# Second feed-forward stage: coefficients in fewer passes, slopes for eight chunks at once, late range marks, idle products, new order

## The chip, the cores and the metric

The kernel runs on one core of a Trainium2 chip. The metric is device time in microseconds (us) of one execution; the kernel before was timed in three runs. TensorE (PE) multiplies; VectorE (DVE), ScalarE (ACT) and GpSimd (POOL) work element by element; SyncE (SP) issues the transfers.

## The reference

Attention over 4 batches of 8 heads (576 tokens, masks of two kinds), then a soft mixture of 8 experts, then a feed-forward layer. The change is in the last of them, on 2304 tokens of width 512:

```
h = x @ w_in                      # x 2304 x 512, w_in 512 x 2048 (float64)
g = h - np.tanh(h)
return (g @ w_out).astype(np.float32)   # w_out 2048 x 512 (float64)
```

Here x is c @ slot_out, with 32 slots, so that h is c times (slot_out @ w_in), and only 32 rows of that product are needed.

## The kernel before

The program has four parts, one after the other: attention (to about 145 us), the dispatch and the experts of the mixture (to about 199 us), and `second`, the feed-forward layer, which is what changes.

`second` reads w_in and w_out as 64-bit words, in 16 pieces i0..i15 (128 columns of w_in) and 16 pieces o0..o15 (128 rows of w_out), 512 KB each, in the order of the list `loads`. Eleven raw buffers take them; a later load waits until a buffer is free again. Each piece is turned into float32 by `low` (ACT or POOL, L774 and L776), `top` (POOL, L779) and `merge` (DVE, L783); `check` (DVE, L787) makes a range mark from it. A raw buffer is free when its merge and its check are done.

The 16 chunks of 128 hidden columns go in nine batches: [0], [1], then pairs. For each batch PE makes a tile p (one buffer): the product of w_in with the slots (L878), to which the marks of the i pieces and of the o pieces loaded so far are added (L883). ACT copies it to g (L887), PE makes the deviations and the means (L891 with `dev`, L893 with `devT`) back into p, ACT takes Gs from it (L898), DVE corrects Gs (L901) and copies GT (L904). Then p is free for the next batch. From GT, POOL makes the coefficients of the batch (`coeffs`, nine operations, L909 and L910) and one slope for each chunk (PT, L935).

The tokens are 18 tiles of 128, in phases: A (tiles 0 to 3), BG (4 to 7), EG (16, 17), C (8 to 11), DG (12 to 15). For each phase and chunk f: PE makes h (L996, 3 buffers), ACT squares it to u with coefficient SC (L1000), DVE makes r from h, u and coefficient BB (L1007, 4 buffers; now and then ACT and POOL, L1011 and L1015), and PE adds r times w_out to the tiles' accumulators acc (L976, 4 buffers), from the rounded copy whi (POOL L856 or ACT L857). Phase A is made while the pieces still arrive. `msum` (L943) sums the slopes times w_out over all chunks; after two more steps it is Ms, and every tile gets one more product with Ms ("affine"). The partial sums of phase A wait in `store` (L1041); their affine products come last of all, and L1059 adds and writes them.

A verdict on the range is worked out on DVE (`judge_b`, L1076 on, and `judge_c`) with one small product between (L1101); it sets a flag that is read at the end, for a slow path that doesn't run here.

The order of all this on each engine is set ahead of time by `Plan`: tasks with durations, dependencies and buffers, placed one by one; on the chip each engine runs its list strictly in order. The attention and the experts keep their own order.

Of the kernel before, what the change touches and what calls it, by code (L numbers as in the profile page):

```python
# [78 lines left out]
class Plan:  # L79

    def __init__(self, bufs):
        self.tasks, self.bufs = [], bufs

    def add(self, *alts, deps=(), take=(), free=(), ready=0.0):
        t = dict(alts=alts, deps=[d for d in deps if d is not None], take=take, free=free, ready=ready, id=len(self.tasks))
        self.tasks.append(t)
        return t

    def run(self, free_at):
        tasks, free_at = self.tasks, dict(free_at)  # L90
# [18 lines left out]

        def earliest(t):  # L110
            s = t["ready"]
            for d in t["deps"]:
                s = max(s, d["end"] + (0.05 if d["eng"] == t["alts"][0][0][0] else 0.2))
            for tag, key in t["take"]:
                k = order.get(tag, [])
                s = max(s, taken.get(tag, -99.0))
                if len(k) >= self.bufs[tag]:
# [3 lines left out]
                    s = max(s, released[old] + 0.1)  # L121
            return s

        while open_:
# [51 lines left out]
def attention_moe_moe(ctx: ExitStack, tc: tile.TileContext, q, k, v, phi, w1, w2, w_in, w_out, cst, out, dbg=None):  # L176
# [20 lines left out]
    big = const.tile([128, NS], F16, name="big")  # L197
    nc.gpsimd.memset(big, 2.0 ** 13)
# [538 lines left out]

    NCK = 8

    def second(raw, chk, cT, store, more):  # L740
# [3 lines left out]
        loads = pieces("i0 o0 i1 o1 i2 i3 o2 o3 i4 i5 o4 o5 i6 i7 o6 o7 i8 i9 o8 o9 i10 i11 o10 o11 i12 i13 o12 o13 i14 i15 o14 o15")  # L744
# [552 lines left out]
```

## Time and profile before

| | |
|---|---|
| three runs | 363.84, 365.88, 366.21 us; median 365.88 |
| the profiled execution | 367.04 us, of which 365.3 us is its span |
| PE, DVE, ACT, POOL busy | 310.7, 244.8, 182.6, 140.2 us |
| granted TensorE clock over the span | 0.919 of full speed |

Times in the trace count from the start of the span. A busy PE is not a PE at its peak, since the matmuls are pipelined and their ends are modelled; a row's idle time is that of its engine just before the instruction, and behind the arrow stands what ended it.

### The profile page before, as it was taken

What the parts mean: (1) busy time and instruction counts of PE and PEld (TensorE: products, weight loads), DVE (VectorE), ACT (ScalarE), POOL (GpSimd) and SP (SyncE); (2) the same over time, 40 slices, a digit from 0 to 9 for tenths busy, and PEclk for the clock granted to TensorE, in tenths of its full rate; (3) what the DMA queues carried; (4) which work ended last, traced back from release to release, by engine and by line L of the source; (5) the groups of instructions that cost most, each with busy time, mean ns of one, the idle gap of its engine ahead of it and who ended that gap; (6) DMA issues with size and microseconds to landing.
All of it is one profiled execution on the core that took longest, in us unless ns stands there. A gap on an engine that the chain in (4) does not pass through costs nothing.

```text
span 365.3 us, 7576 instructions
## 1 busy us (share of the span) xinstructions
PE 310.7 (85%) x2635; PEld 224.2 (61%) x2635; DVE 244.8 (67%) x786; ACT 182.6 (50%) x371; POOL 140.2 (38%) x263
## 2 busy tenths in 40 slices
PE   7996998799999998999997466474889999899990
PEld 4885887588788785643443344352664677676670
DVE  5696697478788875447227765966875568985552
ACT  3364565456586754322214466467265546666520
POOL 0555452636355420015006899989770000110000
PEclk9998899699999999999999655599699999999997
DMA  4677799697889999969999998532000003101106
GB/s 130 159 192 230 203 251 252 160 235 205 223 220 247 241 294 361 358 240 396 410 400 375 374 316 276 174 135 97 2 0 0 2 0 116 60 0 50 65 17 222
DMA packets 52988, 70.20 MB, mean 192 GB/s; under 512 B 22608, under 2 KB 40400, under 8 KB 52944
## 3 DMA queue, kind: packets, MB, share of 16 engines
q1 hardware_dynamic: 52944, 69.65, 60.2%
q8 instruction: 23, 0.38, 0.4%
q14 instruction: 21, 0.17, 0.1%
HBM read 64.91 MB, written 4.72 MB: 191 GB/s over the span
## 4 chain that ended last, share of the span: by engine, by line
PE 34%; POOL 13%; DVE 6%; issue 4%; ACT 1%; DVEq 0%; POOLq 0%; ACTq 0%
PE acc L976 15%; PE h L996 5%; PE hp L689 3%; PE sop L704 3%; POOL co L910 3%; POOL co L909 2%; POOL PT L935 2%; POOL X L779 2%; PE ht L696 2%; PE sp L611 1%; DVE r L1007 1%; PE msum L943 1%; POOL whi L856 1%; PE dt L584 1%; DVE chk_i L787 1%
## 5 line engine op out<-in xcount | busy, mean ns | idle before, releaser
L976 PE MATMUL acc<-whi,r 128*128 128x512 f32 x288 | 83.9, 412 | 4.9 <-DVE r L1007 3.0
L1000 ACT ACTIVATE u<-h,co 128x512 f32<-128x512 f32 (+1 forms) x80 | 51.0, 646 | 34.2 <-PE h L996 31.6
L1007 DVE SCALAR_TENSOR_TENSOR r<-h,co,u 128x512 fp32r<-128x512 f32 (+1 forms) x77 | 52.6, 694 | 19.4 <-PE acc L976 16.1
L976 PEld LDWEIGHTS acc<-whi,r 128*128 128x128 f32 x288 | 54.6, 196 | 17.5 <-DVE r L1007 3.3
L380 PE MATMUL sc<-kT,qbd 128*128 128x96 f32 x272 | 40.0, 288 | 0.5 <-DVE kT L311 0.2
L403 ACT COPY pT<-pp 96x512 f32<-96x512 f32 x38 | 22.2, 584 | 35.5 <-PE pp L402 35.1
L384 DVE CUSTOM_DVE_ANT_0 sm<-sc,m_sb 128x96 f32<-128x96 f32 x144 | 29.4, 260 | 14.8 <-PE sc L380 10.9
L380 PEld LDWEIGHTS sc<-kT,qbd 128*128 128x128 f32 x272 | 35.3, 200 | 3.1 <-issue 2.0
L996 PE MATMUL h<-cT,Gs 128*128 128x512 f32 (+1 forms) x80 | 33.8, 440 | 1.0 <-DVE r L1007 0.9
L255 POOL TENSOR_SCALAR qm<-q 72x512 f32<-72x512 f32 x30 | 20.0, 684 | 29.6 <-PE tr_k L295 11.5
L255 POOL TENSOR_SCALAR km<-k 72x512 f32<-72x512 f32 x30 | 19.6, 669 | 28.7 <-DMA k<-in_k 14.0
L413 PE MATMUL pv<-vw,pT 96*64 96x65 f32 x608 | 27.6, 232 | 3.1 <-POOL vw L278 2.8
L413 PEld LDWEIGHTS pv<-vw,pT 96*64 96x64 f32 x608 | 21.8, 140 | 9.7 <-issue 4.5
L402 PE MATMUL pp<-c_sb,sm 128*96 128x128 f32 x152 | 23.9, 281 | 0.7 <-ACT sm L395 0.7
L388 DVE TENSOR_TENSOR sm<-sm,mx 128x384 f32<-128x384 f32 (+1 forms) x38 | 23.6, 622 | 1.2
L996 PEld LDWEIGHTS h<-cT,Gs 128*128 128x128 f32 x80 | 15.3, 199 | 14.3 <-DVE r L1007 11.0
L1015 POOL TENSOR_TENSOR r<-d,u 128x512 fp32r<-128x512 f32 x3 | 4.3, 1436 | 50.7 <-ACT d L1011 50.7
L878 PE MATMUL p<-X,soT 128*32 128x256 f32 (+1 forms) x72 | 7.3, 488 | 18.3 <-DVE Gs L901 16.2
L395 ACT ACTIVATE sm<-sm 128x384 f32<-128x384 f32 x38 | 19.9, 523 | 3.7 <-DVE sm L388 3.0
L311 DVE COPY kT<-tr_k 128x288 f32<-128x288 f32 x32 | 17.8, 562 | 4.9 <-PE tr_k L295 4.8
L295 PE MATMUL tr_k<-c_sb,km 72*128 72x72 f32 x128 | 16.2, 251 | 5.3 <-POOL km L255 3.1
L302 ACT COPY qbd<-tr_q 64x288 f32<-64x288 f32 x32 | 13.3, 414 | 12.9 <-PE tr_q L295 12.7
(196 smaller groups left out, 583.1 us busy)
## 6 DMA issues: line engine op xcount, KB each, us to landing
w<-in_moe_w SPq DMA_DIRECT2D x60, 512.0 KB
raw_o<-in_moe_w_out SPq DMA_DIRECT2D x16, 512.0 KB
raw_i<-in_moe_w_in SPq DMA_DIRECT2D x15, 512.0 KB
q<-in_q SPq DMA_DIRECT2D x32, 144.0 KB
k<-in_k SPq DMA_DIRECT2D x32, 144.0 KB
out<-X SPq DMA_DIRECT2D x14, 256.0 KB
vw<-in_v SPq DMA_DIRECT2D x16, 144.0 KB
vw<-in_v SPq DMA_DIRECT2D x32, 64.0 KB
```

Of the source, the lines that this page charges most:

```text
L255: nc.gpsimd.tensor_scalar(out=dst, in0=src, scalar1=1.0, scalar2=0.0, op0=ALU.mult, op1=ALU.add)
L380: nc.tensor.matmul(sc[:, o:o + n, :].rearrange("p g k -> p (g k)"), lhsT=qbd[u % NQ][:, j].rearrange("p a n -> p (a n)"), rhs=keys, start= ...
L384: nc.vector.tensor_tensor_reduce(out=sm[:, o:o + n, :].rearrange("p g k -> p (g k)"), in0=sc[:, o:o + n, :].rearrange("p g k -> p (g k)"), ...
L388: nc.vector.tensor_tensor(out=sm[:, o:o + n], in0=sm[:, o:o + n], in1=mx[:, o:o + n].unsqueeze(2).to_broadcast([128, n, KB]), op=ALU.subtract)
L395: nc.scalar.activation(out=st[b], in_=st[b], func=AF.Exp, scale=0.125)
L402: nc.tensor.transpose(pp[:, i, :], sm[:, i, :], ident)
L403: nc.scalar.copy(pT, pp)
L413: nc.tensor.matmul(pv[64 * ab:64 * ab + 64, i, :], lhsT=pT[:, o + x, 64 * ab:64 * ab + 64], rhs=w[:, ab, u % 2, j + x, :], start=x == 0, s ...
L976: nc.tensor.matmul(live[key], lhsT=lhsT(), rhs=rhs(), start=new, stop=stop)
L996: nc.tensor.matmul(live["h", key], lhsT=Gs[:, 128 * f:128 * (f + 1)], rhs=cT[:, c0:c0 + w], start=True, stop=True)
L1000: nc.scalar.activation(out=live["u", key], in_=live["h", key], func=AF.Square, scale=co[:, SC, f:f + 1])
L1007: nc.vector.scalar_tensor_tensor(out=live["r", key], in0=live["h", key], scalar=co[:, BB, f:f + 1], in1=live["u", key], op0=ALU.add, op1=A ...
```

## The change

- **Coefficients.** `coeffs` has five POOL operations for a batch where there were nine. GT is copied by ACT, unclamped, where DVE copied and clamped it. Factors of 8, 5 and 1/8 go into `dev`, `devT`, SC, whi and the copies that are made anyway.
- **Slopes.** The 16 operations of L935 are replaced by two calls of `slope`, for eight chunks each: five small operations and two of 128x256.
- **Late marks.** The check of o8 to o15 moves behind Ms, with a product of its own for each piece (`marks`, eight of 128x512) and one reduction, ahead of `judge_b`.
- **Idle products.** In phase A four products of 128x512 that nobody reads go ahead of each h, into the same buffer.
- **Constants.** `dev`, `devT` and `big` are made when the loads start, in the tile `more`.
- **Order.** i8 to i15 are loaded ahead of o8 to o15; the planner has other durations and hand-over times, takes buffers in the order in which tasks were added, and has boosts; r has 5 buffers; the alternative of ACT and POOL for r is never taken (`POOLR`). The affine products of phase A go in between instead of last, and the last phase ends tile by tile.

```diff
-        loads = pieces("i0 o0 i1 o1 i2 i3 o2 o3 i4 i5 o4 o5 i6 i7 o6 o7 i8 i9 o8 o9 i10 i11 o10 o11 i12 i13 o12 o13 i14 i15 o14 o15")
+        loads = pieces("i0 o0 i1 o1 i2 i3 o2 o3 i4 i5 o4 o5 i6 i7 o6 o7 i8 i9 i10 i11 i12 i13 i14 i15 o8 o9 o10 o11 o12 o13 o14 o15")
...
+        dev, devT, big = more[:, 3 * DM:3 * DM + 128], more[:, 3 * DM + 128:3 * DM + 161], more[:, 3 * DM + 161:].bitcast(F16)
...
-        plan = Plan(dict(raw=RAW, chk=NCK, h=3, p=1, acc=4, u=3, r=4, d=2, g1=1, o=8))
+        plan = Plan(dict(raw=RAW, chk=NCK, h=3, p=1, acc=4, u=3, r=5, d=2, g1=1, o=8))
...
+                late = kind == "o" and f >= 8
+                if not late:
+                    ck = add(one("DVE", 0.55, lambda piece=piece: check(piece)), deps=[ld], take=[("chk", piece)], free=[("raw", piece)])
...
                 def gt_copy():
-                    nc.vector.tensor_scalar(out=GT[:, f0:f0 + n, :], in0=live["p", f0][:, 256:256 + 33 * n].rearrange("p (n x) -> p n x", n=n), scalar1=GMAX, scalar2=-GMAX, op0=ALU.min, op1=ALU.max)
+                    nc.scalar.copy(GT[:, f0:f0 + n, :], live["p", f0][:, 256:256 + 33 * n].rearrange("p (n x) -> p n x", n=n))
...
-                    tt(c(S2), h0, h0)
-                    ts(c(SC), c(S2), -2.0 * 3 ** -0.5, 3 ** -0.5)
-                    ts(c(TMP), c(S2), 8.0, 3.0)
-                    tt(c(BB), c(TMP), h0)
-                    ts(c(A1), c(S2), -2.0 / 3.0, 1.0)
-                    tt(c(A1), c(A1), c(S2))
-                    ts(c(TMP), c(S2), -2.0 / 15.0, 1.0 / 3.0)
-                    tt(c(TMP), c(TMP), c(S2))
-                    tt(c(A0), c(TMP), h0)
+                    nc.gpsimd.tensor_scalar(out=c(H0), in0=GT[:, f0:f0 + n, NS], scalar1=GMAX, scalar2=-GMAX, op0=ALU.min, op1=ALU.max)
+                    nc.gpsimd.tensor_tensor(out=c(S2), in0=c(H0), in1=c(H0), op=ALU.mult)
+                    nc.gpsimd.tensor_scalar(out=c(SC), in0=c(S2), scalar1=-16.0 * 3 ** -0.5, scalar2=8.0 * 3 ** -0.5, op0=ALU.mult, op1=ALU.add)
+                    nc.gpsimd.tensor_scalar(out=c(TMP), in0=c(S2), scalar1=0.375, scalar2=1.0, op0=ALU.add, op1=ALU.mult)
+                    nc.gpsimd.tensor_tensor(out=c(BB), in0=c(TMP), in1=c(H0), op=ALU.mult)
...
-                P["pt", x] = add(one("POOL", 0.2, lambda x=x: nc.gpsimd.tensor_scalar(out=PT[:, x, :], in0=GT[:, x, 0:NS], scalar1=co[:, A1, x:x + 1], scalar2=co[:, A0, x:x + 1], op0=ALU.mult, op1=ALU.add)), deps=[cf])
+        def slope(x):
+            fs = slice(8 * x, 8 * x + 8)
+            c = lambda k: co[:, k, fs]
+            nc.gpsimd.tensor_scalar(out=c(A1), in0=c(S2), scalar1=-1.5, scalar2=1.0, op0=ALU.add, op1=ALU.mult)
...
+            wide = lambda k: c(k).unsqueeze(2).to_broadcast([128, 8, NS])
+            nc.gpsimd.tensor_tensor(out=PT[:, fs, :], in0=GT[:, fs, 0:NS], in1=wide(A1), op=ALU.mult)
+            nc.gpsimd.tensor_tensor(out=PT[:, fs, :], in0=PT[:, fs, :], in1=wide(A0), op=ALU.add)
...
+                    idle = 4 if phase_no == 0 else 0
...
+                        for _ in range(idle):
+                            nc.tensor.matmul(live["h", key], lhsT=cT[:, 0:128], rhs=cT[:, c0:c0 + w], start=True, stop=True)
...
+        def marks(f):
...
+            nc.tensor.matmul(live["oc"][0:1, :], lhsT=big[:, 0:1], rhs=chks["o", f].bitcast(F16), start=f == 8, stop=f == NF - 1)
...
+            ck = add(one("DVE", 0.55, lambda f=f: check(("o", f))), deps=[P["mg", ("o", f)], ready_m], take=[("chk", ("o", f))], free=[("raw", ("o", f))])
```

Three places show what the order does. On POOL, where the coefficients and slopes of the middle batches stand (L909, L910 coefficients and L935 slope before; L932 to L936 coefficients, L956 to L963 the slopes of eight chunks after; L779 and L799 the tops of pieces, X for w_in and wof for w_out, L856 the rounded copy), before:

```order
L910 TENSOR_TENSOR co<-GT 128x2
L909 TENSOR_SCALAR co<-co 128x2 x2
L910 TENSOR_TENSOR co<-co,GT 128x2
L909 TENSOR_SCALAR co<-co 128x2
L910 TENSOR_TENSOR co<-co 128x2
L909 TENSOR_SCALAR co<-co 128x2
L910 TENSOR_TENSOR co<-co 128x2
L910 TENSOR_TENSOR co<-co,GT 128x2
L779 TENSOR_SCALAR X_76<-raw_i_3331 128x512
L935 TENSOR_SCALAR PT<-GT,co 128x32 x4
L1015 TENSOR_TENSOR r_6_0_3408<-d_6_0_3406,u_6_0_3388 128x512
```

and now, for batch 8 and the first eight chunks:

```order
L932 TENSOR_SCALAR co<-GT 128x2
L933 TENSOR_TENSOR co<-co 128x2
L934 TENSOR_SCALAR co<-co 128x2
L935 TENSOR_SCALAR co<-co 128x2
L936 TENSOR_TENSOR co<-co 128x2
L956 TENSOR_SCALAR co<-co 128x8
L957 TENSOR_TENSOR co<-co 128x8
L958 TENSOR_SCALAR co<-co 128x8
L959 TENSOR_TENSOR co<-co 128x8
L960 TENSOR_TENSOR co<-co 128x8
L962 TENSOR_TENSOR PT<-GT,co 128x256
L963 TENSOR_TENSOR PT<-PT,co 128x256
```

Four of nine operations for a batch are gone, the slopes have left the batch, and the two wide operations stand once for eight chunks.

On PE, behind the marks of the batch of chunks 4 and 5 (h is named by phase tile, so h_2_0 is chunk 2 of phase A; p by batch), before:

```order
L996 MATMUL h_2_0_3208<-cT,Gs 128x512
L996 MATMUL h_3_0_3210<-cT,Gs 128x512
L891 MATMUL p_3182<-g_4_3212,dev 128x256
L893 MATMUL p_3182<-devT,g_4_3212 128x33 x2
L878 MATMUL p_3255<-X_76,soT 32x256 x4
```

and now:

```order
L1033 MATMUL h_2_0_3161<-cT 128x512 x4
L1034 MATMUL h_2_0_3161<-cT,Gs 128x512
L1033 MATMUL h_3_0_3168<-cT 128x512 x4
L1034 MATMUL h_3_0_3168<-cT,Gs 128x512
L915 MATMUL p_3137<-g_4_3179,more 128x256
L917 MATMUL p_3137<-more,g_4_3179 128x33 x2
L1009 MATMUL acc_0_3065<-whi,r_1_0_3177 128x512
L1009 MATMUL acc_1_3070<-whi,r_1_0_3177 128x512
```

Eight idle products stand between the marks and the `dev` product of the batch, and accumulations of chunk 1, which before came ahead, stand behind it.

On PE, at the very end, before (acc_0 to acc_3 of the affine products belong to phase A; acc_12 to acc_15 are the tiles of the last phase):

```order
L976 MATMUL acc_12_4296<-whi,r_15_12_4425 128x512
L976 MATMUL acc_13_4302<-whi,r_15_12_4425 128x512
L976 MATMUL acc_14_4307<-whi,r_15_12_4425 128x512
L976 MATMUL acc_15_4319<-whi,r_15_12_4425 128x512
L976 MATMUL acc_0_4445<-Ms,cT 128x512
L976 MATMUL acc_1_4450<-Ms,cT 128x512
L976 MATMUL acc_2_4452<-Ms,cT 128x512
L976 MATMUL acc_3_4456<-Ms,cT 128x512
```

and now:

```order
L1009 MATMUL acc_15_4286<-whi,r_12_12_4414 128x512
L1009 MATMUL acc_12_4275<-whi,r_15_12_4432 128x512
L1009 MATMUL acc_13_4277<-whi,r_15_12_4432 128x512
L1009 MATMUL acc_14_4281<-whi,r_15_12_4432 128x512
L1009 MATMUL acc_15_4286<-whi,r_13_12_4418 128x512
L1009 MATMUL acc_15_4286<-whi,r_14_12_4427 128x512
L1009 MATMUL acc_15_4286<-whi,r_15_12_4432 128x512
```

The four affine products have left the end, and the last three products all belong to tile 15, so tiles 12 to 14 are complete before them.

## Rows read from the trace of the kernel before

**Rows 1.** The page: the span, and the granted clock in 40 slices.

```profile
span 365.3 us, 7576 instructions
...
PEclk9998899699999999999999655599699999999997
```

**Rows 2.** Windows: stretch, its length, busy time (instructions) by engine, clock, DMA.

```profile
198.80:275.30 76.50, 48.21 (x335) 33.82 (x333) 55.74 (x97) 42.51 (x74) 65.83 (x141) 0.73 0.51 175
275.30:354.80 79.50, 78.44 (x340) 54.13 (x339) 54.16 (x113) 44.35 (x75) 2.57 (x2) 1.00 0.10 34
```

**Rows 3.** A window inside the first of these; same columns.

```profile
215.00:225.00 10.00, 6.38 (x38) 4.36 (x38) 6.50 (x13) 6.88 (x11) 9.37 (x19) 0.50 0.86 283
```

**Rows 4.** Waits, 198.8 to 275.3: waiter, releaser, total us, times, longest.

```profile
PE p L878 <- DVE Gs L901: 16.2, 5, 6.3
DVE X L783 <- POOL X L779: 8.2, 6, 3.3
PE p L891 <- POOL dev L811: 4.6, 1, 4.6
```

**Rows 5.** Groups of POOL, 198.8 to 275.3: busy, mean ns, idle.

```profile
L779 POOL TENSOR_SCALAR X<-raw_i 128x512 bf16<-128x512 int16 x14 | 11.8, 861 | 0.1
L909 POOL TENSOR_SCALAR co<-co 128x2 f32<-128x2 f32 (+1 forms) x36 | 10.5, 290 | 2.8
L935 POOL TENSOR_SCALAR PT<-GT,co 128x32 f32<-128x32 f32 x16 | 9.1, 580 | 0.3
...
L910 POOL TENSOR_TENSOR co<-GT 128x2 f32<-128x2 f32 (+1 forms) x9 | 3.2, 358 | 1.3 <-DVE GT L904 1.1
```

**Rows 6.** Tile views of raw_i and raw_o: ns min/median/max, first and last start.

```profile
L783 DVE SCALAR_TENSOR_TENSOR X<-raw_i,X x16: 673/702/1176, 194.2 to 255.1; 128x512 int32<-128x512 int32 x16
...
L787 DVE TENSOR_SCALAR chk_o<-raw_o x16: 408/433/1004, 196.3 to 258.8; 128x512 uint16<-128x512 uint16 x16
```

**Rows 7.** Groups of DVE and ACT, same stretch.

```profile
L1007 DVE SCALAR_TENSOR_TENSOR r<-h,co,u 128x512 fp32r<-128x512 f32 x18 | 13.1, 747 | 1.5 <-ACT u L1000 0.8 <-POOL co L909 0.5
L901 DVE TENSOR_TENSOR Gs<-p,Gs 64x256 fp32r<-64x256 f32 (+1 forms) x9 | 3.6, 398 | 0.3
...
L1000 ACT ACTIVATE u<-h,co 128x512 f32<-128x512 f32 x21 | 13.9, 686 | 6.0 <-PE h L996 4.5 <-POOL co L909 1.5
L774 ACT ACTIVATE X<-raw_i,wround 128x512 int16<-128x512 uint16 x12 | 10.1, 865 | 0.0
```

**Rows 8.** Timeline of PE: start, length; two batches, at either clock.

```profile
222.49 1.08 PE L878 MATMUL p<-X,soT 128*32 128x256 f32 x8 [1.60 <-POOL co L909]
233.05 1.08 PE L878 MATMUL p<-X,soT 128*32 128x256 f32 x8 [6.35 <-DVE Gs L901]
237.65 0.72 PE L891 MATMUL p<-g,dev 128*128 128x256 f32 x2
240.01 0.64 PE L878 MATMUL p<-X,soT 128*32 128x256 f32 x8 [0.49 <-POOL co L909]
241.84 0.59 PE L891 MATMUL p<-g,dev 128*128 128x256 f32 x2
242.27 0.53 PE L893 MATMUL p<-devT,g 128*128 128x33 f32 x4
```

**Rows 9.** Timeline of DVE: the merge of i3; first and last row of judge_b.

```profile
202.69 1.18 DVE L783 SCALAR_TENSOR_TENSOR X<-raw_i,X 128x512 int32<-128x512 int32 x1
...
313.83 0.68 DVE L1076 TENSOR_TENSOR gsq<-GT 128x512 f32<-128x512 f32 x1
...
318.69 0.17 DVE L1097 TENSOR_REDUCE ok<-scw 128x1 f32<-128x16 f32 x1
```

**Rows 10.** The chain that ended last: start, length, what.

```profile
275.38 3.57 PE msum L943 x32
349.19 5.17 PE acc L976 x22
357.38 0.68 DVE X L1059
```

More of the change, by code (lines that the diff above doesn't have):

```diff
@@ L91, in run @@
         users, users_left, left, order, released = [[] for _ in tasks], [0] * len(tasks), {}, {}, {}
+        gives, takes = {}, {}
+        for t in tasks:
+            for x in t["free"]:
+                gives.setdefault(x, []).append(t)
+            for x in t["take"]:
+                takes[x] = t
+        for tag, keys in self.ordered.items():
+            for k in range(self.bufs[tag], len(keys)):
+                t = takes[tag, keys[k]]
+                t["deps"] = t["deps"] + [g for g in gives[tag, keys[k - self.bufs[tag]]] if g not in t["deps"]]
         for t in tasks:
@@ L843, in second @@
             if piece not in early["low"]:
-                lo = add(one("ACT", 0.9, lambda piece=piece: low(piece, True)), one("POOL", 0.95, lambda piece=piece: low(piece, False)), deps=[ld] + busy)
+                lo = add(one("ACT", 0.88, lambda piece=piece: low(piece, True)), one("POOL", 0.92, lambda piece=piece: low(piece, False)), deps=[ld] + busy)
             if piece not in early["top"]:
-                tp = add(one("POOL", 0.95, lambda piece=piece: top(piece)), deps=[ld] + busy)
+                tp = add(one("POOL", 0.87, lambda piece=piece: top(piece)), deps=[ld] + busy)
             if piece not in early["merge"]:
-                mg = add(one("DVE", 0.95, lambda piece=piece: merge(piece)), deps=[ld, lo, tp], free=[("raw", piece)])
-                ck = add(one("DVE", 0.45, lambda piece=piece: check(piece)), deps=[ld], take=[("chk", piece)], free=[("raw", piece)])
+                mg = add(one("DVE", 0.85, lambda piece=piece: merge(piece)), deps=[ld, lo, tp], free=[("raw", piece)])
+                late = kind == "o" and f >= 8
+                if not late:
+                    ck = add(one("DVE", 0.55, lambda piece=piece: check(piece)), deps=[ld], take=[("chk", piece)], free=[("raw", piece)])
             else:
@@ L865, in second @@
             if f0 == batches[-1][0]:
-                outs_ = [x for x in loads if x[0] == "o" and ("in", x) not in P]
+                outs_ = [x for x in loads if x[0] == "o" and x[1] < 8 and ("in", x) not in P]
             for x in outs_:
@@ L1059, in fin @@
                         nc.vector.tensor_tensor(out=live["o", t], in0=live[k], in1=part(t), op=ALU.add)
[L1061 removed]
+                    z = add(one("DVE", 0.69, fin), deps=[chain[t], lastA], take=[("o", t)], free=[fk], boost=40.0)
                 add(one("OUT", 0.7, lambda t=t: write(t, live["o", t])), deps=[z], free=[("o", t)])
@@ L1120, in second, with judge_o @@
         j = add(one("DVE", 0.2, judge_a), deps=[j], free=[("p", "km")])
-        j = add(one("DVE", 4.0, judge_b), deps=[j] + emaxes + [P["co", f] for f in range(NF)])
+        def marks(f):
+            if f == 8:
+                live["oc"] = ps.tile([128, 512], F32, tag="p", name="marks", bufs=1)
+            nc.tensor.matmul(live["oc"][0:1, :], lhsT=big[:, 0:1], rhs=chks["o", f].bitcast(F16), start=f == 8, stop=f == NF - 1)
+        def judge_o():
+            nc.vector.tensor_reduce(out=okt[:, 6:7], in_=live["oc"][0:1, :], axis=AX.X, op=ALU.max)
+        mk_ = j
+        for f in range(8, NF):
+            ck = add(one("DVE", 0.55, lambda f=f: check(("o", f))), deps=[P["mg", ("o", f)], ready_m], take=[("chk", ("o", f))], free=[("raw", ("o", f))])
+            mk_ = add(one("PE", 0.22, lambda f=f: marks(f)), deps=[ck, mk_], take=[("p", "oc")] if f == 8 else [], free=[("chk", ("o", f))])
+        mk_ = add(one("DVE", 0.6, judge_o), deps=[mk_], free=[("p", "oc")])
+        j = add(one("DVE", 4.0, judge_b), deps=[j, mk_] + emaxes + [P["co", f] for f in range(NF)])
         j = add(one("PE", 0.2, verdict), deps=[j], take=[("p", "vd")])
```

94 lines of the change are left out of this document (56 added, 38 removed).

## The prediction

> **What bounds the kernel now.** I read the page first. Of 367.04 us the span takes 365.3 and 1.7 lie around it [rows 1]; the median of the three runs, 365.88, is 1.2 below the profiled time, so I take the gain from the trace and subtract it from the median. The clock row falls to half in the middle of the program [rows 1]: that is the first part of the second stage, so I cut the stage by windows. From 198.8 to 275.3, while the pieces arrive, POOL is busy 65.8 of 76.5 us, DVE 55.7, PE 48.2 at a mean clock of 0.73; transfers fill half of it. From 275.3 to 354.8 PE is busy 78.4 of 79.5 us [rows 2]. So POOL sets the first stretch and PE the second. The waits say how: PE's start of a batch waits 16.2 us for the correction of Gs on DVE, DVE's merges wait 8.2 us for POOL's tops, and the first batch 4.6 us for `dev` [rows 4]. The correction is short, 0.40 us [rows 7], but it stands in DVE's list behind merges whose tops are late. POOL's list carries 81 coefficient operations (45 of them in the two groups shown) and 16 slopes, which cost 9.1 us although they are small [rows 5].
>
> **First stretch, POOL.** Of 81 coefficient operations 36 go. The two groups average 0.29 and 0.36 us [rows 5]; at 0.29 that is 10.4 us. The slopes take 9.1 away; a call of `slope` has five small operations, 1.5 us at 0.29, and two of 128x256 that no row shows. Their bounds are a 128x32 operation, 0.58, and a whole top of 128x512, 0.86 [rows 5]; they read two inputs, so I take 0.8, 3.1 for a call (2.6 to 3.2). Only the first call lies in the stretch; the second comes after POOL's last piece, ahead of `msum`. `dev` and its two neighbours, 1.1 at 0.36, leave for a stretch in which POOL still waits for the first pieces. By the order, rounded copies go from eight to six and five lows come from ACT; at 0.86, the price of a top of the same size, that is -1.7 and +4.3. Sum: 65.8 - 10.4 - 9.1 + 3.1 - 1.1 - 1.7 + 4.3 = 50.9.
>
> **First stretch, DVE, ACT and PE.** DVE loses eight checks, at 0.43 to 1.00 each [rows 6] say 4.6, and nine GT copies, which go to ACT, each at most 0.40 like the correction that reads the same tile [rows 7]. PE gets 64 idle products. At full clock a product of 512 columns takes 0.235 (22 in 5.17 [rows 10]), so 15.0 us; at half clock 30. The rest of PE's list to the last acc of phase A is nine batches of about 2.0 (less for the first two, 17 together) and 64 acc and 21 h at 0.235, 20. So PE needs 52 at full clock, POOL 51, and DVE 55.7 - 4.6 less its GT copies, about 49: none sets the length alone any more, and I follow the lists instead.
>
> **The walk, by starts of the batches.** Prices: merge 0.8, check 0.5, between median and longest [rows 6]; low and top 0.86 [rows 5, 7]; r 0.75, u 0.69, the correction of Gs 0.40, Gs and GT the same on ACT [rows 7]; a batch's own products 2.8 from 240.01 to the end of 242.27 + 0.53 at full clock, of which PE works some 2.0 [rows 8]; an idle group with its h 1.2. Before, batches 4, 6 and 8 start at 222.5, 233.05 and 240.0 [rows 8].
> - Batch 1 starts at 204.3: no wait for `dev`, but the first correction of Gs still stands behind the merge of i3, which ended at 203.9 ([rows 9], 202.69 + 1.18) and does not move.
> - Batch 2, 6.1 later: at half clock the five products ahead of `dev` cost 2.4, and ACT has a u and a low (1.55) ahead of Gs. Batch 4, 5.5 later: DVE's three merges, three checks and a Gs with its correction, 4.7, behind batch products already at full clock. That is 215.9.
> - Batch 6, 6.0 later: four merges, three checks, one r, 5.5, then the correction. 221.9.
> - Batch 8, 7.9 later: POOL does five coefficient operations, four tops and two lows, 6.6, and two merges can only follow. 229.8.
> - Batch 10, 4.0 later: POOL's next low and four tops, 4.3, of which the first fits in before, then the last merge. Batch 12, 6.6: three idle groups with h 3.6, the products 2.0, four acc 0.9. 240.4.
> - Batch 14, 7.0: PE's first products and an idle group, 2.1, then ACT's u, low, Gs, GT and low in a row, 3.2, then a merge, a check and the correction, 1.7. 247.4.
> - From here PE alone decides: batch 2.0, four idle groups with h 4.8, five h more and 36 acc 9.6, in all 16.4: 263.8 for the last acc of phase A.
>
> I add 1.8 for hand-overs and for POOL and DVE being busy at once more than before: `msum` begins at 265.6 and not at 275.4 [rows 10]. That is -9.8. The second `slope` call hides behind those 16 us; without them it would cost its 3.1. Copies in `store` hide behind `msum` as before.
>
> **Second stretch.** Counted by the order, PE has from `msum` on 283 products of 512 columns after, 284 before up to 354.4 (end of the second of [rows 10]). To these come `msum` 3.6, 16 half-width h, and small ones, about 6.7 together, and now eight marks, 1.9. Before: 284 x 0.235 + 6.7 = 73.4, in 79.0 us, so 5.6 us of stalls. After: 66.5 + 6.7 + 1.9 = 75.1. The stalls before come of h and acc in uneven groups and r in four buffers; after, the list has one h after every four acc, and five buffers of r. Against that, DVE gets late checks, and `judge_b` now stands before the last four r, with the small product that waits for it ahead of the last h (318.69 + 0.17 - 313.83 = 5.0 before [rows 9]). I leave 2.7 of stalls (1 to 5). The end: before, 354.4 to 358.06 ([rows 10], 357.38 + 0.68) for four evictions, four affine products and four adds; after, the affine products are in the count and one copy of 0.7 with its hand-over, 0.95, is left. The 7.2 us from there to the span's end I leave. So 75.1 + 2.7 + 0.95 + 7.2 = 85.95, before 365.3 - 275.4 = 89.9: -3.9.
>
> Sum: 365.3 - 9.8 - 3.9 = 351.6 of span, 353.3 with the 1.7 around it; from the median, 352.2.
>
> **Clock.** The walk takes full clock from about 212 on. The rows: after an idle stretch of 6.35 us PE began batch 6 at 233.05 at half clock (its product group takes 1.08), worked through, and at 237.65 the `dev` product had fallen to 0.72 on its way to 0.59; batch 8 takes 0.64 [rows 8]. So steady work brings the 2.4 GHz level, and what falls away here are pauses of that length. In a window in which PE worked 6.4 of 10 us it stayed at 0.50 [rows 3].
> The Trainium skill's "TensorE: Matmul & The Clock Gate", section "HAM oscillation — how this bites in real kernels", says that a kernel whose matmuls pause for operands falls back to half clock again and again; by that rule the idle products must fill each pause to be worth anything. [rows 3] agrees for the kernel before.
>
> **Rivals.**
> - *The clock stays at half and the idle products become the bound* (slower). Place: the groups ahead of `dev` and Gs in phase A. PE's 52 us grow as one over the clock. The second stretch gives 3.9, so it decides from where they pass 80.4 us, at a mean clock of 0.65; at 0.60 they take 87, which gives 372, and at 0.50 104, which gives 389. For it speaks [rows 3]; against it that the gaps of the walk are under 3 us where the clock fell after 4.6 and 6.35 [rows 4, 8].
> - *POOL and DVE slow each other.* A merge took from 0.67 to 1.18, a check from 0.41 to 1.00 [rows 6]. With both engines nearly always busy, 29 merges and 21 checks could cost 0.3 and 0.35 more than I took, 16 us on DVE; half of it on the path gives 360, all of it about 366, no change.
> The Trainium skill's "GPSIMD Engine Reference", section "8. Key points", says that POOL shares its SBUF interfaces with DVE and contends with DVE instructions that have two SBUF inputs; the merge is one. [rows 6] agrees that the same shape varies so, not that POOL is the cause.
> - *The stage is shorter but the rest gives it back*: marks, late checks and `judge_b` stall PE by 6 more than I left; 358.
> - *Better*: full clock from the start and merges at their median of 0.70 take another 6 us off: 346.
>
> **How the numbers follow.** Forecast with its surroundings (348 to 357) 0.52; better (below 348) 0.13; contention or stalls that leave 357 to 362, 0.17; within 1%, which is about what a measurement of this kernel can tell from no change (362.2 to 369.5), 0.09; slower 0.09. So faster 0.82, same 0.09, slower 0.09. Cutting 5 in 100 below and 15 above gives 343 to 365; the forecast's own range is 348 to 357.
>
> **What would show it.** Right: `msum` near 265, POOL under 52 us busy ahead of it, clock near 0.9 in 215 to 260, the first wait of batch 1 under 1 us, last acc less than 1.5 us before the last copy. Wrong: a clock of half past 225; waits of a batch for DVE still over 10 us in all; merges at a mean over 1.0; gaps of PE over 2 us each behind `judge_b`.

## The result and the profile after

The changed kernel takes 354.56 us (median of 4 runs, 352.29 to 355.87) against 365.1 us of the kernel before (4 runs, 363.84 to 366.21): a ratio of 0.971, 95% interval 0.964 to 0.977. The forecast was 352.2 us, in a range of 343 to 365. The profiled execution takes 354.68 us, its span 352.8 [rows 1]; the page, span and granted clock in 40 slices:

```profile
span 352.8 us, 7610 instructions
...
PEclk9999999899995899999999969978999999999998
```

The half clock in the middle of [rows 1] is gone, but for a dip to 0.6 and one to 0.7. The stage in two windows, up to `msum` and behind it (columns as in [rows 2]):

```profile
198.80:267.80 69.00, 56.88 (x393) 42.73 (x393) 56.27 (x86) 44.27 (x86) 56.06 (x103) 0.90 0.61 202
267.80:346.00 78.20, 76.59 (x346) 56.30 (x345) 57.89 (x128) 42.19 (x71) 0.00 (x0) 1.00 0.15 49
```

POOL has 103 instructions and 56.1 us where it had 141 and 65.8 [rows 2]. PE is 8.7 us busier in a stretch that is shorter, since 20.1 us of idle products are in it. The batches on PE (start, length, idle time before) and the start of `msum` (the sum over the slopes), to be set beside [rows 8] and [rows 10]:

```profile
200.69 0.43 PE L902 MATMUL p<-X,soT 128*32 128x128 f32 x8
205.50 0.66 PE L902 MATMUL p<-X,soT 128*32 128x128 f32 x8 [2.50 <-DVE Gs L925]
211.22 0.64 PE L902 MATMUL p<-X,soT 128*32 128x256 f32 x8
215.78 0.64 PE L902 MATMUL p<-X,soT 128*32 128x256 f32 x8 [1.13 <-POOL co L933]
222.25 0.64 PE L902 MATMUL p<-X,soT 128*32 128x256 f32 x8 [1.27 <-POOL co L935]
229.81 0.64 PE L902 MATMUL p<-X,soT 128*32 128x256 f32 x8 [0.28 <-DVE X L803]
235.50 1.08 PE L902 MATMUL p<-X,soT 128*32 128x256 f32 x8 [3.24 <-POOL co L936]
243.85 0.64 PE L902 MATMUL p<-X,soT 128*32 128x256 f32 x8
250.35 0.64 PE L902 MATMUL p<-X,soT 128*32 128x256 f32 x8 [0.50 <-DVE Gs L925]
267.84 0.63 PE L976 MATMUL msum<-more,PT 128*32 128x512 f32 x3
```

The wait for `dev` [rows 4] is gone. The longest wait, 3.24 us, is put down to a coefficient, on which this product does not depend; DVE's list shows what it is (the tops are POOL's, start and length):

```profile
231.39 3.50 DVE L803 SCALAR_TENSOR_TENSOR X<-raw_i,X 128x512 int32<-128x512 int32 x4
234.92 0.43 DVE L925 TENSOR_TENSOR Gs<-p,Gs 64x256 fp32r<-64x256 f32 x1
```

```profile
229.26 3.94 POOL L799 TENSOR_SCALAR X<-raw_i 128x512 bf16<-128x512 int16 x4
```

The correction of Gs for batch 8 stands behind four merges, which follow four tops in a row. The end, PE and then DVE's last copy:

```profile
341.11 0.50 PE L1034 MATMUL h<-cT,Gs 128*128 128x512 f32 x1 [0.38 <-DVE r L1045]
341.45 3.82 PE L1009 MATMUL acc<-whi,r 128*128 128x512 f32 x16
```

```profile
345.31 0.69 DVE L1092 COPY X<-acc 128x512 f32<-128x512 f32 x1 [0.38 <-PE acc L1009]
```

From the last accumulation, 345.27, to the end of the last copy, 346.0, pass 0.73 us, where it was 3.7 [rows 10].

Now and then an execution is disturbed and takes some per cent longer; the ratios below leave such executions out, the medians do not, and the lengths of d_gs0 are not shown because the profiled one was such.

### The profile page after: what moved, and what is told of

Same layout as the page of the kernel before. It is cut to its first block, busy times and chain, and to the rows that moved or that the text cites. A ratio compares the mean times of both kernels' runs of the same rounds, so it can differ in the third digit from the quotient of the medians.

```text
span 352.8 us, 7610 instructions
## 1 busy us (share of the span) xinstructions
PE 314.7 (89%) x2675; PEld 233.8 (66%) x2675; DVE 244.4 (69%) x783; ACT 180.0 (51%) x375; POOL 127.8 (36%) x225
## 4 chain that ended last, share of the span: by engine, by line
PE 36%; POOL 6%; DMA 5%; DVE 5%; ACT 2%; issue 2%; ACTq 0%; DVEq 0%; POOLq 0%
PE acc L1009 17%; PE h L1034 4%; PE h L1033 4%; DMA w<-in_moe_w 3%; DMA raw_o<-in_moe_w_out 3%; POOL X L799 2%; PE hp L707 2%; PE sp L629 1%; DVE r L1045 1%; PE p L902 1%; PE msum L976 1%; PE ht L714 1%; POOL X L796 1%; ACT u L1038 1%; PE dt L602 1%
## 5 line engine op out<-in xcount | busy, mean ns | idle before, releaser
L1009 PE MATMUL acc<-whi,r 128*128 128x512 f32 x288 | 80.1, 398 | 1.4 <-DVE r L1045 1.1
L1038 ACT ACTIVATE u<-h,co 128x512 f32<-128x512 f32 (+1 forms) x80 | 50.9, 647 | 44.2 <-PE h L1034 37.4
L1045 DVE SCALAR_TENSOR_TENSOR r<-h,co,u 128x512 fp32r<-128x512 f32 (+1 forms) x80 | 55.0, 695 | 24.8 <-PE acc L1009 16.0
L1009 PEld LDWEIGHTS acc<-whi,r 128*128 128x128 f32 x288 | 52.5, 188 | 15.9 <-issue 2.4
L1034 PE MATMUL h<-cT,Gs 128*128 128x512 f32 (+1 forms) x80 | 30.4, 386 | 0.9 <-DVE r L1045 0.8
L273 POOL TENSOR_SCALAR km<-k 72x512 f32<-72x512 f32 x30 | 19.4, 661 | 27.6 <-DMA k<-in_k 24.5
L420 PE MATMUL pp<-c_sb,sm 128*96 128x128 f32 x152 | 24.9, 289 | 0.7 <-ACT sm L413 0.7
L1033 PE MATMUL h<-cT 128*128 128x512 f32 x64 | 20.1, 440 | 0.0
L320 ACT COPY qbd<-tr_q 64x288 f32<-64x288 f32 x32 | 13.2, 414 | 12.9 <-PE tr_q L313 12.6
L420 PEld LDWEIGHTS pp<-c_sb,sm 128*96 128x96 f32 x152 | 17.1, 135 | 2.3 <-ACT sm L413 1.0
```

The costliest lines, as they stand in the source:

```text
L273: nc.gpsimd.tensor_scalar(out=dst, in0=src, scalar1=1.0, scalar2=0.0, op0=ALU.mult, op1=ALU.add)
L420: nc.tensor.transpose(pp[:, i, :], sm[:, i, :], ident)
L1009: nc.tensor.matmul(live[key], lhsT=lhsT(), rhs=rhs(), start=new, stop=stop)
L1033: nc.tensor.matmul(live["h", key], lhsT=cT[:, 0:128], rhs=cT[:, c0:c0 + w], start=True, stop=True)
L1034: nc.tensor.matmul(live["h", key], lhsT=Gs[:, 128 * f:128 * (f + 1)], rhs=cT[:, c0:c0 + w], start=True, stop=True)
L1038: nc.scalar.activation(out=live["u", key], in_=live["h", key], func=AF.Square, scale=co[:, SC, f:f + 1])
```

## The experiments

All kernels side by side. The last three columns come from the one profiled execution of each: the start of the first product of chunk 0, the time from there to `msum`, and from there to the span's end. The stage's start scatters from 195.1 to 202.6 although next to nothing ahead of it differs, so the two lengths are compared and not points in time. Three kernels that have the changed kernel's order up to `msum` (itself, the old end, POOL busy) show 67.1, 68.6 and 66.6: some 2 us is the scatter of one profiled execution. The profiled executions of a_idle0 (355.16 us) and a_idle8f (358.22 us) were the longest of their kernels, 2.7 and 2.2 above the median.

| kernel | us, median | ratio to before (interval) | start | to msum | to the end |
|---|---|---|---|---|---|
| before | 365.1 | 1 | 199.0 | 76.3 | 90.0 |
| changed | 354.56 | 0.971 (0.964 to 0.977) | 200.7 | 67.1 | 85.0 |
| a_idle0 | 352.51 | 0.963 (0.956 to 0.970) | 200.7 | 66.9 | 85.6 |
| a_idle8f | 356.06 | 0.973 (0.964 to 0.982) | 202.6 | 69.0 | 84.8 |
| b_idle4 | 371.05 | 1.016 (1.008 to 1.023) | 197.5 | 81.6 | 89.7 |
| a_slopes9 | 362.45 | 0.994 (0.990 to 0.998) | 195.1 | 77.1 | 84.4 |
| b_slopes2 | 357.62 | 0.983 (0.976 to 0.990) | 195.3 | 68.2 | 90.2 |
| a_gtdve | 354.59 | 0.972 (0.965 to 0.979) | 201.1 | 67.3 | 84.4 |
| a_earlychk | 356.36 | 0.978 (0.972 to 0.985) | 196.5 | 70.9 | 86.5 |
| a_endold | 353.55 | 0.965 (0.957 to 0.973) | 197.6 | 68.6 | 86.1 |
| a_r4 | 354.39 | 0.971 (0.963 to 0.978) | 196.3 | 69.4 | 85.8 |
| a_poolidle | 350.24 (one run) | | 197.4 | 66.6 | 84.4 |
| c_actlow | 348.89 | 0.955 (0.948 to 0.961) | 199.1 | 61.1 | 87.5 |
| d_gs0 | 345.86 | 0.944 (0.937 to 0.950) | | | |

**No idle products (a_idle0).**

```diff
-                    idle = 4 if phase_no == 0 else 0
+                    idle = 0
```

> The changed kernel with none of its 64 idle products; every other instruction stands where it stood. Theory (the idle products keep TensorE at its 2.4 GHz level while the pieces arrive): the granted clock of 205 to 245 falls back towards 0.5, a batch's products take 1.08 us again instead of 0.64, the sum over the slopes begins 3 to 7 us later than 267.8, and the time is 357 to 362 us. Rival (they only fill TensorE, which is 9.5 to 9.7 of 10 us busy from 235 to 265, with 20.1 us that nobody reads): the sum begins 2 to 5 us earlier, the time is 350 to 353 us. If both are about equal, 353.5 to 356.5.

The clock did fall, and the stretch did not get longer: 66.9 us to `msum`. In windows, the stretch to `msum` and 205 to 245:

```profile
198.80:267.60 68.80, 49.69 (x331) 34.93 (x331) 55.18 (x85) 43.77 (x86) 57.83 (x103) 0.80 0.61 203
...
205.00:245.00 40.00, 29.92 (x215) 21.00 (x216) 34.06 (x53) 23.30 (x47) 34.19 (x67) 0.71 0.85 280
```

Without its 20.1 us of idle products PE is busy 49.7 us and not 56.9: what it does for the result took 36.8 us in the changed kernel and takes 49.7 here, at a mean clock of 0.80. The idle products bought 12.9 us of PE for 20.1 us of PE, on an engine that is not the limit there. The changed kernel's clock from 205 to 245 is 0.86. My theory fell. Between the rival and the third case the run does not decide: the median, 352.51, lies in the rival's 350 to 353 and 2 us under the changed kernel's, with intervals that overlap, but the start of `msum` moved by 0.2 us and not by 2 to 5. A gain from leaving the idle products out is thus possible and not shown; a loss is not there.

**Idle products in front of the first eight h only (a_idle8f).**

```diff
-                    idle = 4 if phase_no == 0 else 0
+                    idle = 4 if phase_no == 0 and f < 8 else 0
```

> The changed kernel with idle products only ahead of the first eight h of phase A, 32 instead of 64; every other instruction stands where it stood. By the walk TensorE alone sets the pace from the batch of chunks 12 and 13 on, so that the eight groups of 0.93 us left out, 7.4 us, are worth something until DVE or POOL, 8.3 of 10 us busy there, set it: the sum begins 2 to 4 us earlier, 351 to 353 us. Rival (DVE and POOL set the pace there already): within 1 us of the changed kernel, 354 to 356 us. Rival (the clock falls behind the last idle group): the clock of 245 to 265 is below 0.8 and the time 356 us or more.

No gain: the 7.4 us taken out of PE's list behind batch 10 are worth nothing that can be measured. In the windows from 245 to 265 of this kernel POOL is busy 8.4 and 9.2 of 10 us, PE 7.6 and 7.1. The clock there is 1.00, so the last rival's condition does not hold either, though its time does (356.06, within the scatter). So PE alone did not set the end of the walk, as I had it. What it waits for there shows in a_idle0, where PE has room (start, length, idle time before):

```profile
256.82 1.20 PE L1009 MATMUL acc<-whi,r 128*128 128x512 f32 x4 [1.70 <-ACT whi L881]
...
262.36 1.81 PE L1009 MATMUL acc<-whi,r 128*128 128x512 f32 x4 [1.96 <-POOL whi L880]
```

The rounded copies of the last pieces come late, behind their tops on POOL and merges on DVE.

**The kernel before with idle products (b_idle4).** The two lines of the idle loop, as in the change's diff, in the kernel before.

> The kernel before with the four idle products ahead of each h of phase A and nothing else of the change. Theory (POOL, 65.8 of 76.5 us busy, sets the first stretch of the kernel before, and the clock is second): the clock of the stretch rises from 0.73 to about 0.9, but the start of the sum moves by 0 to 3 us; 362 to 366 us. Rival (the clock was most of the loss): the sum begins 5 us or more earlier, 357 to 360 us. Rival (the products take the place of real work): 367 us or more.

The last case came: 371.05 us, 81.6 us to `msum` and not 76.3, at a mean clock of 0.83 where the kernel before has 0.73. POOL's work is the same, 64.9 us. That the products delay the chain of a batch, since they stand ahead of its `dev` product in PE's list, is how I read it, and not shown.

**POOL's work put back (a_slopes9).**

```diff
                     nc.gpsimd.tensor_tensor(out=c(BB), in0=c(TMP), in1=c(H0), op=ALU.mult)
+                    nc.gpsimd.tensor_scalar(out=c(A1), in0=c(S2), scalar1=-1.5, scalar2=1.0, op0=ALU.add, op1=ALU.mult)
+                    nc.gpsimd.tensor_tensor(out=c(A1), in0=c(A1), in1=c(S2), op=ALU.mult)
...
+                    for x in range(f0, f0 + n):
+                        nc.gpsimd.tensor_scalar(out=PT[:, x, :], in0=GT[:, x, 0:NS], scalar1=co[:, A1, x:x + 1], scalar2=co[:, A0, x:x + 1], op0=ALU.mult, op1=ALU.add)
...
-            pt = add(one("POOL", 3.2, lambda x=x: slope(x)), deps=[P["co", f] for f in range(8 * x, 8 * x + 8)])
+            pt = add(one("POOL", 3.2, lambda: None), deps=[P["co", f] for f in range(8 * x, 8 * x + 8)])
```

> The changed kernel with POOL's work put back into the batches: after the five coefficient operations of a batch come the five small ones of the slope for that batch and a 128x32 slope operation for each chunk, and the two calls for eight chunks are gone. The rest stands where it stood. POOL gets 9 times 5 small operations at about 0.27 and 16 at about 0.58, less the 5.6 us of the two calls: 15.8 us more, 56 to 72 us busy. Theory (POOL's relief is the largest part of the gain): the sum over the slopes begins 6 to 10 us later, 360 to 365 us. Rival (DVE's list and the idle products set the pace and POOL has 13 us to spare): 1 to 4 us later, 355 to 359 us.

```profile
195.10:272.10 77.00, 59.10 (x370) 43.58 (x369) 52.33 (x81) 43.27 (x83) 65.53 (x149) 0.87 0.52 171
```

POOL is back at 65.5 us (I had 72) and the stretch at 77.1, about the length of the kernel before (76.3), with early constants, idle products, GT on ACT, late checks and the new order all in place. The theory's stretch and time, 362.45 us, hold. That the rest of the change is worth nothing does not follow: b_idle4 has the same idle products, and against its 81.6 this kernel is 4.5 shorter.

**The relief alone, in the kernel before (b_slopes2).** In `coeffs` of the kernel before the five operations from A1 on go, and the 16 operations of L935 become two calls:

```diff
+        def slope(x):
+            fs = slice(8 * x, 8 * x + 8)
...
+            nc.gpsimd.tensor_tensor(out=PT[:, fs, :], in0=GT[:, fs, 0:NS], in1=wide(A1), op=ALU.mult)
+            nc.gpsimd.tensor_tensor(out=PT[:, fs, :], in0=PT[:, fs, :], in1=wide(A0), op=ALU.add)
```

> The kernel before with POOL's relief alone: a batch keeps four coefficient operations (S2, SC, TMP, BB), and the other five and the 16 slope operations become two calls for eight chunks, as in the changed kernel. The planner's order around them moves a little. Nothing else of the change is in it. Theory (POOL's list sets the first stretch, so this part alone brings most of the gain): from the first product of chunk 0 to the sum over the slopes it takes 67 to 71 us where the kernel before took 76.3 and the changed one 67.1, and the time is 356 to 361 us. Rival (the relief helps only together with the checks, copies and order of the change): 73 us or more, 362 to 366 us.

```profile
195.30:263.50 68.20, 45.98 (x332) 32.14 (x331) 58.43 (x96) 42.58 (x74) 49.38 (x91) 0.77 0.57 194
```

This one part gives 8.1 of the 9.2 us that the first stretch lost, at a clock of 0.77. Its second stretch, 90.2 us, is that of the kernel before (90.0), so the 5.0 us there come of the rest.

**GT on DVE again (a_gtdve).**

```diff
-                    nc.scalar.copy(GT[:, f0:f0 + n, :], live["p", f0][:, 256:256 + 33 * n].rearrange("p (n x) -> p n x", n=n))
+                    nc.vector.tensor_copy(GT[:, f0:f0 + n, :], live["p", f0][:, 256:256 + 33 * n].rearrange("p (n x) -> p n x", n=n))
```

> The changed kernel with the nine copies of GT made by DVE instead of ACT, at the same places of the order. DVE gets 9 at about 0.25 to 0.40, 2.3 to 3.6 us, just ahead of the correction of Gs for which TensorE waits. Theory (the copy's move was worth what lies ahead of the corrections on the path): the stretch to the sum is 1 to 3 us longer than 67.1, 355.5 to 357.5 us. Rival (hidden: DVE waits there for the copy anyway, 1.5 us in three places): within 1 us of the changed kernel, 353.5 to 355.5 us.

Hidden, as the rival has it: 354.59 us, 67.3 us to `msum`.

**Checks while phase A runs (a_earlychk).** `late` is false, the early check of o8 to o15 has a boost of 200, and the marks product waits for that check and not for a late one. Seven of the eight then come ahead of `msum`, and that of o15 at 325.0; the planner's order moves with them.

```diff
-                late = kind == "o" and f >= 8
+                late = False
...
-            ck = add(one("DVE", 0.55, lambda f=f: check(("o", f))), deps=[P["mg", ("o", f)], ready_m], take=[("chk", ("o", f))], free=[("raw", ("o", f))])
+            ck = P["ck", ("o", f)]
```

> The changed kernel with the checks of o8 to o14 made as soon as the pieces are there, while phase A runs (that of o15 stays behind Ms); the marks products stay where they were. DVE gets seven checks at 0.4 to 1.0, about 4.4 us, in the stretch from 243 to 268 where it is busy 8 of 10 us, and loses them in the second stretch. Theory (POOL and not DVE sets the pace there): the stretch to the sum grows by 0 to 1.5 us and the second stretch is unchanged, 354 to 356 us. Rival (DVE is on the path there): 2 to 4 us longer, 356 to 359 us.

70.9 us to `msum`, 2.3 more than the longest of the three equal ones; the median is 1.8 us above the changed kernel's, with intervals that overlap. It points to the rival, that DVE is on the path there too, but does not settle a size.

**The old end (a_endold).** The entry of `phases` for the affine products of A goes back behind DG, and the boosts of those products, of their adds and of the last phase are 0.

> The changed kernel with the old end: the affine products of phase A and their four adds come last of all again, and the last phase no longer ends tile by tile; the rest of the second stretch keeps its order. Theory (the end was worth 3.66 us from the last accumulation to the last add before, and one copy of 0.7 now): from the sum to the span's end it takes 1.5 to 3 us more than 85.0, 356 to 357.5 us. Rival (evictions and adds follow one another as fast as the four products come, so that only the products are moved): 0 to 1 us more, 354 to 355.5 us.

86.1 us from `msum` to the end against 85.0, and no slower in time: the rival. The tail that the new end saves reappears as products inside the list.

**Four r buffers (a_r4).** `r=5` becomes `r=4` in the planner and `bufs=5` becomes `bufs=4` in `r_new`; the order moves with them, ahead of `msum` too.

> The changed kernel with four buffers of r instead of five, in the pool and in the planner, whose order moves with it. Theory (the stalls of TensorE in the second stretch of the kernel before, 5.6 us against 0.8 now, came of r buffers and uneven groups): TensorE's idle time behind the sum rises by 1 to 3 us, 355.5 to 357.5 us. Rival (one h after every four accumulations is what removed them): less than 0.7 us more, 354 to 355.5 us.

The rival again: PE's waits behind `msum` are 1.2 us, 0.8 in the changed kernel, and the median is 354.39 us. The expectation sets these 0.8 beside 5.6 of the kernel before, but that is another measure, a length less a count of products. Counted as waits, the kernel before has 0.9 between `msum` and the last accumulation.

**POOL busy where it is idle (a_poolidle).**

```diff
+        for _ in range(60):
+            add(one("POOL", 0.75, lambda: nc.gpsimd.tensor_scalar(out=PT, in0=GT[:, :, 0:NS], scalar1=8.0, scalar2=0.0, op0=ALU.mult, op1=ALU.add)), deps=[ready_m])
```

> The changed kernel with 60 operations of 128x512 on POOL behind Ms, where POOL has nothing to do; they write slopes that nobody reads any more. The order of the first stretch is unchanged, that behind Ms moves a little. In the changed kernel the late checks of o8 to o15 on DVE took 0.42 us each there, and in the first stretch the same operation took 0.41 to 1.0. Theory (POOL and DVE wait for each other's operations on SBUF): with POOL busy the late checks and gsq take up to 1.1 us, 0.6 or more on average for the checks, and POOL's operations lie between 0.6 and 1.2; the operations that read the product banks (r, the copies of acc) keep their 0.75 and 0.69. Rival (the long ones come of the transfers or of DVE's own list): the checks stay at 0.42. The time by either: 353 to 356 us, since DVE has room there.

The 60 operations (POOL) and the first four late checks (DVE); the other four come after 310.4 and take 0.41 or 0.42:

```profile
267.85 42.51 POOL L989 TENSOR_SCALAR PT<-GT 128x512 f32<-128x512 f32 x60 [4.87 <-PE msum L976]
```

```profile
284.00 0.42 DVE L807 TENSOR_SCALAR chk_o<-raw_o 128x512 uint16<-128x512 uint16 x1
284.53 0.64 DVE L807 TENSOR_SCALAR chk_o<-raw_o 128x512 uint16<-128x512 uint16 x1
...
306.45 0.53 DVE L807 TENSOR_SCALAR chk_o<-raw_o 128x512 uint16<-128x512 uint16 x1
308.77 0.42 DVE L807 TENSOR_SCALAR chk_o<-raw_o 128x512 uint16<-128x512 uint16 x1
```

Two of the four are longer, by 0.22 and 0.11, and the mean is 0.50 where I expected 0.6 or more; r and the copies keep their 0.75 and 0.69. The sign is the theory's and the size is not. The two long ones began while an operation of POOL ran and ended 0.28 us behind its end (284.89 and 306.70), which is how the long checks of the first stretch end too (last section). `gsq` ran when POOL was done, at 332.5, so it tests nothing. The time, 350.24, is under the expected 353 to 356; 3.3 us of it are an earlier start of the stage, and one run says only that DVE has room.

**All lows and rounded copies on ACT (c_actlow).** On top of a_idle0, the planner's POOL alternatives for `low` and for whi are taken out, so ACT makes all that the planner places.

```diff
-                lo = add(one("ACT", 0.88, lambda piece=piece: low(piece, True)), one("POOL", 0.92, lambda piece=piece: low(piece, False)), deps=[ld] + busy)
+                lo = add(one("ACT", 0.88, lambda piece=piece: low(piece, True)), deps=[ld] + busy)
```

> The changed kernel without idle products, and with more taken off POOL: the lows and the rounded copies that the planner gave to POOL (eight lows at 0.93, four copies at 0.79, 10.6 us) are all made by ACT, busy 44 of 69 us; the planner's order moves with them. Theory (POOL sets the pace, 9.0 to 9.4 of 10 us busy in most windows): POOL's busy time falls from 56 to about 45 us, the stretch to the sum from 67 to 61 to 64 us, and the time is 347 to 351 us. Rival (DVE, 56 us, and its merges set the pace as much): less than 1.5 us, 351.5 to 354 us. Rival (ACT, 55 us by then, delays g, Gs and u): 355 us or more.

```profile
199.10:260.20 61.10, 45.88 (x297) 30.11 (x296) 50.44 (x79) 46.10 (x90) 47.26 (x90) 0.80 0.64 217
260.20:341.00 80.80, 78.98 (x356) 58.06 (x355) 58.89 (x129) 45.37 (x77) 0.00 (x0) 1.00 0.14 49
```

The theory holds: POOL 47.3 us, the stretch 61.1, the time 348.89 us. Against a_idle0 the first stretch is 5.8 shorter and the second 1.9 longer, because 56 and not 64 accumulations of phase A, and 21 and not 23 h, lie ahead of `msum`: ten products of 0.235. So some 3.9 us are gained and the rest is moved; the medians differ by 3.6. POOL now waits for GT, 6.5 us in five places; that the chain of a batch is the next limit is how I read it, and not shown.

**The correction of chunk 0 ahead of the merge of i3 (d_gs0).** On top of c_actlow:

```diff
-                mg = add(one("DVE", 0.85, lambda piece=piece: merge(piece)), deps=[ld, lo, tp], free=[("raw", piece)])
+                mg = add(one("DVE", 0.85, lambda piece=piece: merge(piece)), deps=[ld, lo, tp, P["G", 0] if piece == ("i", 3) else None], free=[("raw", piece)])
```

> The kernel without idle products and with all lows and rounded copies on ACT, with one edge more: the merge of i3 on DVE waits until the correction of Gs for chunk 0 is made, so that TensorE's start of chunk 1, which waited 3.0 us for it, comes earlier; the planner's order behind it moves a little. Theory (behind the relief of POOL, the chain of a batch, over g, GT and the coefficients, for which POOL waited 6.5 us, sets the pace): the start of chunk 1 comes 1 to 2 us earlier, the sum 0.5 to 2 us earlier, 347 to 348.5 us. Rival (POOL and DVE make it up later in any case): 348.5 to 350 us.

345.86 us, the fastest of all; but its interval overlaps that of c_actlow, and the mechanism did not come about: chunk 1 still waits 2.9 us for the correction, since the planner put the check of i3 in the place of its merge. The lists behind it differ too. I take it as at least no worse, and the reason of a gain as open.

## Why the prediction was right, point by point

In the profiled execution the forecast of 353.3 missed 354.7 by 1.4: the stage began 1.7 later than before (scatter), the first stretch took 67.1 where the walk has 265.6 - 199.0 = 66.6, the second 85.0 and not 85.95, and 1.9 and not 1.7 lie around the span. The medians differ by 10.5 us and not by the forecast 13.7; the stage itself lost 9.2 + 5.0 = 14.2 in the two profiles. The difference is the later start, 1.7, the 0.2 around the span, and the 1.9 by which the profiled execution of before, 367.04, was above the median of 365.1.

**POOL's relief: right, and the decisive step.** a_slopes9 and b_slopes2 show it from both sides. Its busy time was mis-sized, 56.1 and not 50.9: both `slope` calls lie in the stretch, 5.1 together and not 3.1; the tops, which the sum left as they were, took 26.9 for 30 where they had 24.5 for 29; 36 coefficient operations less gave 9.2 and not 10.4; two rounded copies less gave 1.0 and not 1.7. One term was left out that goes the other way: the r of 1.7 that POOL made before. The unknown price, two inputs of 128x256, was 0.61 to 0.62, near the lower bound of 0.58; I took 0.8.

**The clock and the idle products: the premise held, but was not needed.** The walk has full clock from 212 on, and the trace shows 0.92 from 215 to 260. But a_idle0 gets the same length at 0.71 from 205 to 245, where the changed kernel has 0.86. The first rival did not come: the clock was 0.90, and a_idle0 shows no more than 0.2 us of the stretch lost to the idle products.

**The walk.** Its starts were 204.3, 210.4, 215.9, 221.9, 229.8, 233.8, 240.4, 247.4; measured 205.5, 211.2, 215.8, 222.3, 229.8, 235.5, 243.9, 250.4. Two steps failed. From batch 8 to 10 I had one merge after POOL's tops, and it was four of 0.87 ahead of the correction: 5.7 and not 4.0. Behind that pause of 3.24 us the clock was at half (a product group of 1.08 at 235.50; 0.74 on average from 235 to 245), and the next step, with three idle groups, took 8.4 and not 6.6; a_idle0, with the same 1.08 and no idle products, took 6.3. That PE alone decides behind batch 14 is refuted: a_idle8f has 7.4 us less of it and is no shorter, and a_idle0 starts batch 14 2.4 us earlier, counted from the stage's start, and `msum` only 0.2. So the length agrees within 0.5 us in part by luck. Batch 14 came 1.3 late (49.7 from the stage's start and not 48.4), the margin of 1.8 for hand-overs made it up, and the end has another cause than the one the walk gives it.

**DVE and ACT.** The move of GT is hidden (a_gtdve). The late checks are worth something between nothing and 4 us (a_earlychk). Merges at 0.93 on average instead of 0.8 show the second rival at work in part, 29 times 0.13 or 3.8 us on DVE. (Its upper price was added wrongly: 352.2 and 16 make 368, not 366.)

**The second stretch.** By the terms: PE's counted work to the last accumulation 75.1, what is left of the length 77.4 - 75.1 = 2.3 (forecast 2.7), the last copy 0.73 (0.95), the tail 352.8 - 346.0 = 6.8 (7.2). The sum was right. What the prediction calls stalls, 5.6 before and 2.3 after, is mostly not waiting, for the waits are 0.9 and 0.8 us. It lies in the steps around an h: from the start of an accumulation to that of a full-width h behind it the trace of before has 0.278 us on average (38 times, 12 of them over 0.26) and that of after 0.229 (38, none over 0.26); from an h to an accumulation 0.270 (40) and 0.235 (33). That is some 3.2 us, about the fall from 5.6 to 2.3. a_r4 has 0.229 and 0.241 with four buffers of r, so the fifth is not the reason, and the old end changes nothing that can be measured. By elimination the even order, one h after four accumulations, remains; it was not tried alone, so the cause of the 5.0 us of this stretch, a third of the gain, stays open. The third rival did not come: PE waits 0.8 us behind `msum` in all.

**The markers.** Right: the clock, the last copy, merges under 1.0, no long gap behind `judge_b`. `msum` came at 267.8 and not near 265, of which 1.7 is the later start. Wrong: POOL under 52 us, and a first wait of batch 1 under 1 us (2.5, for the correction, which the walk itself had behind the merge of i3).

## What to carry to other kernels

Cost small operations on a shared, nearly full engine first: nine passes over 128x2 for each batch and a slope for each chunk took 32 of POOL's 65.8 us here, and doing about half of the passes, and the slopes, for eight chunks at once gave 8.1 of the 9.2 us of the first stretch's gain. When clock and waits look bad together, fill the engine only if its own work is on the path: here products that nobody reads raised the clock and bought nothing, and in the kernel before they cost 5.8 us. A sum that comes out is no proof of its reasons: the end of the walk came out in its length, and not for the reason given. Compare lengths from the stage's own start, not points in time, when the program ahead of it scatters by some us.

## What the runs showed of the hardware

In the first stretch merge and check have two lengths. Of the changed kernel's 30 merges from 198.8 on, 16 had 128x512 operations of POOL beside them for more than half their time and took 1.12 on average (0.67 to 1.23); the 13 that had none took 0.67 to 0.69; r, which reads a product bank, took 0.74 or 0.75 in either case. Five rows of DVE, and POOL at the same times:

```profile
213.38 1.00 DVE L807 TENSOR_SCALAR chk_o<-raw_o 128x512 uint16<-128x512 uint16 x1
...
217.98 1.19 DVE L803 SCALAR_TENSOR_TENSOR wof<-raw_o,wof 128x512 int32<-128x512 int32 x1
...
243.38 0.68 DVE L803 SCALAR_TENSOR_TENSOR wof<-raw_o,wof 128x512 int32<-128x512 int32 x1
...
254.15 0.92 DVE L803 SCALAR_TENSOR_TENSOR wof<-raw_o,wof 128x512 int32<-128x512 int32 x1
...
310.02 0.42 DVE L807 TENSOR_SCALAR chk_o<-raw_o 128x512 uint16<-128x512 uint16 x1
```

```profile
213.14 0.96 POOL L799 TENSOR_SCALAR wof<-raw_o 128x512 bf16<-128x512 int16 x1
...
217.71 2.09 POOL L799 TENSOR_SCALAR X<-raw_i 128x512 bf16<-128x512 int16 x2
...
244.15 0.62 POOL L880 TENSOR_SCALAR whi<-wof 128x512 fp32r<-128x512 f32 x1 [1.26 <-DVE wof L803]
...
253.82 0.78 POOL L796 TENSOR_SCALAR wof<-raw_o 128x512 int16<-128x512 uint16 x1
```

The lengths follow the end of POOL's operation. Of the 17 merges that began while one of 128x512 ran, 15 were long, and each of them ended 0.47 to 0.54 us behind its end (the merge at 254.15: 255.07 and 254.60); the other two met only its last 0.06 and 0.13. Seven checks that began so took 0.66 to 1.02, and each ended 0.28 behind it.

It goes both ways: POOL's five operations for a batch took 0.19 each at their shortest, and this one, beside the merge from 241.60 to 242.29, took 0.59 and ended at 242.34:

```profile
241.75 0.59 POOL L934 TENSOR_SCALAR co<-co 128x2 f32<-128x2 f32 x1
```

```profile
241.60 0.69 DVE L803 SCALAR_TENSOR_TENSOR wof<-raw_o,wof 128x512 int32<-128x512 int32 x1
```

So in these rows the one that begins later waits for the other's end, and a short operation costs what it meets. The Trainium skill's "SBUF — State Buffer", section "Who interferes with whom", says so: a contending DVE operation and one of POOL hold a shared pair of ports for a whole instruction, and the later one waits. The trace agrees: in the last pair, and in the 15 merges and seven checks, of which the check at 213.38 is one (it ends at 214.38, the top that began before it at 214.10). POOL's relief did not make these meetings fewer for DVE: merges of more than 0.8 us are 9 of 29 in the kernel before, 8 in b_slopes2 and 15 in the changed kernel, at a mean of 0.82, 0.82 and 0.93. What the meetings cost in time on the path was not measured.
